# Softplus operations of the first group given a priority 250 instructions ahead, in a fused attention and mixture-of-experts kernel

## The chip, the cores and the metric

The kernel runs on one core of a Trainium2 chip. The metric is the device time of one execution in microseconds, the median over several runs; lower is better.

## What is computed

The reference is a chain of three stages over 4608 tokens of width 512.

```python
# 1. attention, keys and values averaged over windows of 8 (72 of 576 stay)
scores = q @ mean8(k).T / 8;  attn = softmax(scores);  x = attn @ mean8(v)
# 2. a dense layer with softplus
h = x @ w_in                                    # 512 -> 2048
g = maximum(h, 0) + log1p(exp(-abs(h)))
x = g @ w_out                                   # 2048 -> 512
# 3. tokens with x @ w_skip > 0 go through one of 8 experts (argmax of x @ w_gate)
h = maximum(x @ w1[e], 0);  out = x + gate * (h @ w2[e])
```

## The kernel before

Stage 2 goes over nine groups of 512 tokens, and in each over 16 chunks of 128 hidden columns. For a chunk, `p1` (L707 to L726) multiplies the group's activations `xh`, `xl` with a slice of `w_in`: 12 matmuls (L715) into one of two PSUM buffers `h`. Operands are split in a high and a low float32 part, and three products are summed. Then come seven instructions, which this text calls the softplus: Abs, Exp and Ln on ScalarE (L718, L719, L720), a combination on VectorE that reads `h` a last time (L721), a copy to the high part `gh` on ScalarE (L723) and the low part `gl` on VectorE (L725). `p2` (L728 to L738) multiplies `gh`, `gl` with a slice of `w_out`: 12 matmuls into the four accumulators `y`. In program order `p2` of a chunk follows `p1` of the chunk two further on. The next `p1` but one can't begin before L721 has read its `h` buffer.

Beside this, while group g is in stage 2, a generator `unit` (L622 to L670) per head pair makes the attention output of group g+1; four head pairs fill the `xh`, `xl` that the next group's `p1` reads, head pair by head pair (`kk` in the loop). One unit goes: load the keys (`kv<-kT`, L624, on SP's queue), reduce them over windows (`kp`, L530), copy them into a block-diagonal tile (`kbd`, L537, L538), scores on TensorE (`s`, L635), maximum and subtraction (L644, L645), Exp on ScalarE (L542), sums and a division, a transposition on VectorE (L653), twelve small copies that finish the transposition (`et<-q`, L659, on SP's queue), the product with the values (`o`, L569), and the split into `xh` (L571, ScalarE) and `xl` (L572, VectorE). The values are loaded (`kv<-vT`, L532), reduced (`vr`, L553), transposed on TensorE (`pv`, L560) and copied (`vp`, L562). There is one buffer each for `kv`, `et`.

While the first group runs, the weights of stage 2 are also unpacked for the first time: loads of 1 MB (L506) and, for each, two unpacking passes on ScalarE (L469, L471), two joins on VectorE (L474, L476), a copy to the high part (L519) and a subtraction (L520). Later groups reuse the tiles.

The order on each engine is not the program's. A scheduler places each instruction by a priority (its place in the program) among those that its model of the machine holds ready at that time; the engines then run what they were given strictly in that order and wait with semaphores. `tc.high_priority(offset=n)` gives the instructions inside it a priority as if they stood n places earlier. Stage 3 is ordered by hand and comes after all groups.

Of the kernel before, what the change touches and what calls it, by code (L numbers as in the profile page):

```python
# [9 lines left out]
F32 = mybir.dt.float32  # L10
F32R = mybir.dt.float32r
# [3 lines left out]
AF = mybir.ActivationFunctionType  # L15
ALU = mybir.AluOpType
# [4 lines left out]
P = 128  # L21
# [5 lines left out]
G = 512  # L27
# [2 lines left out]
XW = 520  # L30
BIG = float(1 << 20)
LAG = 2


@with_exitstack
def tile_kernel(ctx, tc, qT, kT, vT, wbits, w9, w1, w2, out):
    nc = tc.nc
# [382 lines left out]
    with ExitStack() as ph:  # L420
# [3 lines left out]
        gp = ph.enter_context(tc.tile_pool(name="gp", bufs=3))  # L424
        ap = ph.enter_context(tc.tile_pool(name="ap", bufs=2))
# [37 lines left out]
        def load_weights():  # L463
# [15 lines left out]
            def half(c, j, first):  # L479
                wh, wl = (wt[c // 2][:, c % 2, i, j * 512:(j + 1) * 512] for i in range(2))  # L480
                if first:
                    raw = room("raw", 1024, True).bitcast(I32).rearrange("p (a b) -> p a b", b=2)
                else:
                    raw = scratch.tile([P, 512, 2], I32, tag="raw", name="raw")
                nc.sync.dma_start(out=raw.rearrange("p a b -> p (a b)"),
                                  in_=bits[c * P:(c + 1) * P, j * 1024:(j + 1) * 1024])
                lo, hi = raw[:, :, 0], raw[:, :, 1]
                unpack(lo, hi)
                yield
                join(lo, lo, hi)  # L490
                nc.scalar.activation(out=wh, in_=lo.bitcast(F32), func=AF.Copy)
                yield
                nc.vector.tensor_tensor(out=wl, in0=lo.bitcast(F32), in1=wh.bitcast(F32),
                                        op=ALU.subtract)
                yield
# [3 lines left out]
            for c in range(EARLY):  # L499
                for j in range(2 if c >= LAG else 1):  # L500
                    yield from half(c, j, True)
            for i in range(EARLY // 2, 8):
# [14 lines left out]
                for j in range(2):  # L517
# [3 lines left out]
                    yield  # L521
            for c in range(LAG):
                yield from half(c, 1, False)
# [183 lines left out]
        def p1(g, c):  # L707
            xh, xl = X[g]
            w = wt[c // 2][:, c % 2]
            h = ps_h.tile([P, G], F32, tag="h", name="h")  # L710
            n = 0
            for kk in range(4):
                wh, wl = w[:, 0, kk * P:(kk + 1) * P], w[:, 1, kk * P:(kk + 1) * P]
                for l, r in ((wh, xh), (wh, xl), (wl, xh)):
                    nc.tensor.matmul(h, lhsT=l, rhs=r[:, kk, :], start=n == 0, stop=n == 11)  # L715
                    n += 1
            a = ap.tile([P, G], F32, tag="a", name="a")
            nc.scalar.activation(out=a, in_=h, func=AF.Abs)  # L718
            nc.scalar.activation(out=a, in_=a, func=AF.Exp, scale=-1.0)  # L719
            nc.scalar.activation(out=a, in_=a, func=AF.Ln, bias=1.0)  # L720
            nc.vector.scalar_tensor_tensor(out=a, in0=h, scalar=0.0, in1=a, op0=ALU.max, op1=ALU.add)  # L721
            gh = gp.tile([P, G], F32R, tag="gh", name="gh")
            nc.scalar.activation(out=gh, in_=a, func=AF.Copy)  # L723
            gl = gp.tile([P, G], F32R, tag="gl", name="gl")
            nc.vector.tensor_tensor(out=gl, in0=a, in1=gh.bitcast(F32), op=ALU.subtract)  # L725
            return gh, gl  # L726

        def p2(g, c, gh, gl):  # L728
            if c == 0:
                yps[g] = [ps_y.tile([P, D], F32, tag=f"y{t}", name=f"y{t}") for t in range(T)]  # L730
            w = wt[(c + LAG) % 16 // 2][:, (c + LAG) % 2]
            wh, wl = w[:, 0, 512:], w[:, 1, 512:]
# [10 lines left out]
        def ready(c):  # L743
            if c < EARLY:
                return 3 * (2 * c - min(c, LAG)) + 3
            return 3 * (2 * EARLY - LAG) + 6 * ((c - EARLY) // 2) + 6

# [45 lines left out]
        for g in range(NG):  # L793
            if g + 1 < NG:
                feed.start(units_of(g + 1), 6)
            for c in range(16):
                late = c >= EARLY
                while loaded[0] < min(STEPS, ready(c)):
                    weights(1)
                pend.append((g, c, *p1(g, c)))  # L800
                weights(2 if late else 3)
                feed.tick()
                if len(pend) > 2:
                    item = pend.pop(0)
                    p2(*item)
                    if item[1] == 15:
                        ends.append(finish(item[0], yps[item[0]], lambda: ps_a, "pa"))
                if g == NG - 1:
                    last_group(c)
                weights(1 if late else 3)  # L810
                feed.tick()
                if loaded[0] == STEPS and "cm9" not in ws:
                    scratch_cm.__exit__(None, None, None)
                    ws["cm9"] = ctx.enter_context(tc.tile_pool(name="cm9", bufs=1, side="right"))
                    ws["junk"] = ws["cm9"].tile([P, D], BF16, name="junk")
                    fill = ws["cm9"].tile([P, NCOL], I32, tag="fill", name="fill")
                    nc.gpsimd.memset(fill, int(BIG))
                    nc.sync.dma_start(out=tab.rearrange("(p c) b -> p (c b)", p=P), in_=fill)
            assert loaded[0] == STEPS
            while g + 1 < NG and (feed.units or jobs or ends):  # L820
                feed.tick()
# [17 lines left out]
        g = NG - 1  # L839
# [126 lines left out]
def _layout(q, k, v, moe_w_in, moe_w_out, moe2_w_skip, moe2_w_gate, moe2_w1, moe2_w2):  # L966
# [7 lines left out]
    def words(a, b):  # L974
# [3 lines left out]
            a.reshape(a.shape[0] // P, P, n, P).transpose(2, 1, 0, 3).reshape(n, P, -1),  # L978
            np.roll(b.reshape(n, P, -1), LAG, axis=0)], axis=2)).view(np.int64).reshape(n * P, -1)

# [30 lines left out]
```

## Time and profile before

| what | us |
|---|---|
| median of 3 runs (1370.27 to 1371.11) | 1370.47 |
| the profiled execution | 1378.22 |
| its span, first to last instruction | 1376.5 |
| TensorE busy in the span | 1338.4 (97%) |
| VectorE, ScalarE, GpSimd busy | 847.6, 594.6, 309.6 |

TensorE is the bound. It is busy to 90% or more in all of the span's 40 slices but the first two and the last two, so time can be won or lost only where it waits. Of the 38.1 us that it is not busy, 10.7 lie before 20 us, 7.5 between 20 and 140 us, 2.2 between 800 and 1000 us and 17.2 after 1000 us; between 140 and 800 us it has none. The first group is in stage 2 from 35.6 to about 154 us.

### The profile page before, as it was taken

Reading aid. Unit: us, or ns where it says so; the run is one execution under the profiler, and the core shown is the slowest. Engines: PE = TensorE matmul, PEld = TensorE weight load, DVE = VectorE, ACT = ScalarE, POOL = GpSimd, SP = SyncE. Lnnn points to the kernel's source line nnn. Section 1 sums busy time; section 2 is a strip of 40 time slices with the busy share of each in tenths; the row PEclk is TensorE's granted clock in tenths of the full one; section 3 lists DMA queues with packets and bytes.
Section 4 is the critical chain, followed back from the end, with each engine's and each line's share of the span. In section 5 each row is a group of like instructions: output and inputs, shape, how many; then the busy total and the mean of one; then the engine's idle time right before and its main releaser. Section 6 shows DMA issues by size and latency. Waiting matters only on the chain. (4 is left out here: it accounts for less than half of the span.)

```text
span 1376.5 us, 21364 instructions
## 1 busy us (share of the span) xinstructions
PE 1338.4 (97%) x7030; PEld 1114.9 (81%) x7030; DVE 847.6 (62%) x1951; ACT 594.6 (43%) x1076; POOL 309.6 (22%) x374
## 2 busy tenths in 40 slices
PE   6899999999999999999999999999999999999986
PEld 5667877777878778788778778888989898889886
DVE  7997794783974974965956847545645332325254
ACT  6985544544545545455455445541111121114142
POOL 2000012111121121030030120343424243323233
PEclk9999999999999999999999999999999999999998
DMA  8633343241241340431421301513323122225272
GB/s 283 260 115 90 86 136 75 59 130 48 76 125 35 80 129 26 112 106 31 118 70 33 106 13 47 192 39 92 96 70 100 57 76 67 81 61 169 64 269 80
DMA packets 149599, 134.16 MB, mean 97 GB/s; under 512 B 100789, under 2 KB 116789, under 8 KB 146912
## 3 DMA queue, kind: packets, MB, share of 16 engines
q1 hardware_dynamic: 131744, 95.51, 24.0%
q0 software_dynamic: 17728, 37.13, 8.5%
q8 instruction: 59, 0.97, 0.3%
q14 instruction: 68, 0.56, 0.1%
HBM read 166.67 MB, written 29.67 MB: 143 GB/s over the span
## 5 line engine op out<-in xcount | busy, mean ns | idle before, releaser
L715 PE MATMUL h<-xh,wt 128*128 128x512 f32 x1152 | 381.9, 393 | 3.4 <-DVE a L721 3.1
L715 PEld LDWEIGHTS h<-xh,wt 128*128 128x128 f32 x1152 | 217.6, 189 | 51.2 <-DVE a L721 4.9
L894 PE MATMUL h<-xt,w1h 128*128 128x256 f32 x1280 | 229.1, 282 | 4.2 <-ACT w1h L404 1.7
L736 PE MATMUL y<-wt,gh 128*128 128x512 f32 x576 | 233.2, 405 | 0.0
L119 DVE CUSTOM_DVE_ANT_0 junk<-rows,w9b 128x512 bf16<-128x512 f32 x324 | 223.0, 688 | 8.3 <-ACT rows L113 3.2
L715 PE MATMUL h<-xl,wt 128*128 128x512 f32 x576 | 225.7, 392 | 0.0
L737 PE MATMUL y<-wt,gh 128*128 128x512 f32 x576 | 225.4, 391 | 0.0
L738 PE MATMUL y<-wt,gl 128*128 128x512 f32 x576 | 224.7, 390 | 0.0
L894 PEld LDWEIGHTS h<-xt,w1h 128*128 128x128 f32 x1280 | 197.7, 189 | 9.2 <-issue 4.8
L894 PE MATMUL h<-xt,w1l 128*128 128x256 f32 x640 | 180.4, 282 | 3.8 <-issue 2.4
L898 ACT ACTIVATE hs<-h 128x512 fp32r<-128x512 f32 x80 | 47.6, 598 | 307.5 <-PE h L894 170.1
L718 ACT ACTIVATE a<-h 128x512 f32<-128x512 f32 x144 | 85.9, 597 | 184.1 <-PE h L715 172.4
L721 DVE SCALAR_TENSOR_TENSOR a<-h,a 128x512 f32<-128x512 f32 x144 | 98.5, 684 | 101.0 <-ACT a L720 100.4
L723 ACT ACTIVATE gh<-a 128x512 fp32r<-128x512 f32 x144 | 90.8, 630 | 158.5 <-DVE a L721 152.9
L736 PEld LDWEIGHTS y<-wt,gh 128*128 128x128 f32 x576 | 108.1, 188 | 36.5 <-ACT a L718 8.3
L715 PEld LDWEIGHTS h<-xl,wt 128*128 128x128 f32 x576 | 109.0, 189 | 22.9 <-issue 0.7
L738 PEld LDWEIGHTS y<-wt,gl 128*128 128x128 f32 x576 | 108.1, 188 | 23.7 <-DVE gl L725 0.4
L725 DVE TENSOR_TENSOR gl<-a,gh 128x512 fp32r<-128x512 f32 x144 | 99.2, 689 | 42.0 <-ACT gh L723 39.4
L894 PEld LDWEIGHTS h<-xt,w1l 128*128 128x128 f32 x640 | 122.7, 192 | 2.8 <-issue 1.0
L737 PEld LDWEIGHTS y<-wt,gh 128*128 128x128 f32 x576 | 108.3, 188 | 20.1 <-issue 0.4
L920 PE MATMUL y<-w2h,hs 128*128 128x512 f32 x304 | 118.4, 390 | 0.3 <-issue 0.3
L919 PE MATMUL y<-w2l,hs 128*128 128x512 f32 x304 | 118.4, 389 | 0.2 <-issue 0.2
(197 smaller groups left out, 1728.0 us busy)
## 6 DMA issues: line engine op xcount, KB each, us to landing
w9b<-w SPq DMA_DIRECT2D x81, 256.0 KB
raw<-wbits SPq DMA_DIRECT2D x12, 1024.0 KB
x2d<-rows SPq DMA_DIRECT2D x36, 260.0 KB
et<-q SPq DMA_DIRECT2D x256, 32.0 KB
kv<-kT SPq DMA_DIRECT2D x28, 288.0 KB
kv<-vT SPq DMA_DIRECT2D x28, 288.0 KB
xm<-misc SPq DMA_DIRECT2D x160, 32.0 KB
misc<-misc SPq DMA_DIRECT2D x144, 32.0 KB
```

The lines of the kernel that those rows point to most:

```text
L119: nc.vector.tensor_tensor_reduce(out=ws["junk"], in0=rows[t][:, :D], in1=w9b[e], scale=1.0, scalar=0.0, op0=ALU.mult, op1=ALU.add, accum_o ...
L715: nc.tensor.matmul(h, lhsT=l, rhs=r[:, kk, :], start=n == 0, stop=n == 11)
L718: nc.scalar.activation(out=a, in_=h, func=AF.Abs)
L721: nc.vector.scalar_tensor_tensor(out=a, in0=h, scalar=0.0, in1=a, op0=ALU.max, op1=ALU.add)
L723: nc.scalar.activation(out=gh, in_=a, func=AF.Copy)
L725: nc.vector.tensor_tensor(out=gl, in0=a, in1=gh.bitcast(F32), op=ALU.subtract)
L736: nc.tensor.matmul(y, lhsT=th, rhs=wh, start=c == 0, stop=False)
L737: nc.tensor.matmul(y, lhsT=th, rhs=wl, start=False, stop=False)
L738: nc.tensor.matmul(y, lhsT=tl, rhs=wh, start=False, stop=c == 15)
L894: nc.tensor.matmul(h[:, f2, :], lhsT=l, rhs=r[:, kk, :], start=n == 0, stop=n == 11)
L919: nc.tensor.matmul(y, lhsT=hh[:, f, js], rhs=ws["w2l"][:, f, :], start=False, stop=False)
L920: nc.tensor.matmul(y, lhsT=hl[:, f, js], rhs=ws["w2h"][:, f, :], start=False, stop=f == 7)
```

## The change

A constant AHEAD = 250 is added, and in the first group alone (`g == 0`) the seven instructions of a chunk's softplus are given a priority 250 places ahead. Nothing that is computed changes. Lines after the constant move down by one, those from the softplus on by four (L718 is L722 after the change).

```diff
+AHEAD = 250
...
-            a = ap.tile([P, G], F32, tag="a", name="a")
-            nc.scalar.activation(out=a, in_=h, func=AF.Abs)
...
+            with ExitStack() as st:
+                if g == 0:
+                    st.enter_context(tc.high_priority(offset=AHEAD))
+                a = ap.tile([P, G], F32, tag="a", name="a")
+                nc.scalar.activation(out=a, in_=h, func=AF.Abs)
+                nc.scalar.activation(out=a, in_=a, func=AF.Exp, scale=-1.0)
+                nc.scalar.activation(out=a, in_=a, func=AF.Ln, bias=1.0)
+                nc.vector.scalar_tensor_tensor(out=a, in0=h, scalar=0.0, in1=a, op0=ALU.max, op1=ALU.add)
+                gh = gp.tile([P, G], F32R, tag="gh", name="gh")
+                nc.scalar.activation(out=gh, in_=a, func=AF.Copy)
+                gl = gp.tile([P, G], F32R, tag="gl", name="gl")
+                nc.vector.tensor_tensor(out=gl, in0=a, in1=gh.bitcast(F32), op=ALU.subtract)
```

The scheduler makes of it other orders in the first group and at the step to the second; from `p2` of the second group's third chunk on TensorE's order is the old one but for one place.

ScalarE, around the Exp of the second head pair's attention (L542), before:

```order
L469 ACTIVATE raw_768<-raw_768 128x1024
L471 ACTIVATE raw_768<-raw_768 128x1024
L542 ACTIVATE q<-q 128x8x72
L571 ACTIVATE xh<-o 128x512
L538 ACTIVATE kbd_165<-kp 64x72
L723 ACTIVATE gh<-a 128x512
L469 ACTIVATE raw_905<-raw_905 128x1024
```

and after the change (L543 is the Exp, L572 `xh`, L727 `gh`, L722 Abs):

```order
L472 ACTIVATE raw_768<-raw_768 128x1024
L538 ACTIVATE kbd_165<-kp 64x72
L727 ACTIVATE gh<-a 128x512
L572 ACTIVATE xh<-o 128x512
L539 ACTIVATE kbd_165<-kp 64x72
L470 ACTIVATE raw_905<-raw_905 128x1024
L722 ACTIVATE a<-h 128x512
L543 ACTIVATE q<-q 128x8x72
L723 ACTIVATE a<-a 128x512
```

The Exp now stands behind `gh`, `xh`, a `kbd` copy, an unpacking pass and an Abs that it stood ahead of.

SP's queue, at the load of the keys of the third head pair (L624), before:

```order
L506 DMA raw_905<-wbits 128x2048 x2
L624 DMA kv<-kT 128x576
L659 DMA et<-q 32x8x32 x2
L659 DMA et<-q 8x8x32
L659 DMA et<-q 32x8x32 x2
```

and after (L625 is the load of the keys):

```order
L660 DMA et<-q 8x8x32
L660 DMA et<-q 32x8x32 x2
L660 DMA et<-q 8x8x32
L625 DMA kv<-kT 128x576
L626 DMA q<-qT 128x64
L626 DMA q<-qT 128x448
```

The load went from ahead of the second head pair's twelve copies to behind them. The load of the keys of the first unit for the third group moved in the same way, from ahead of the fourth head pair's copies to behind them.

TensorE, from the last `p1` matmuls of the second chunk of group 1 to `p2` of the first group's last chunk, before:

```order
L715 MATMUL h<-xl,wt_181 128x512
L715 MATMUL h<-xh,wt_181 128x512
L635 MATMUL s<-kbd_165,q 128x144
L635 MATMUL s<-kbd_167,q 128x144 x3
L736 MATMUL y_551<-wt_181,gh 128x512
```

and after, from the end of that `p2` to the beginning of the third chunk's `p1` (L570 is `o`, L636 `s`, L716 `p1`, L561 `pv`):

```order
L570 MATMUL o<-et,vp 64x64 x2
L636 MATMUL s<-kbd_165,q 128x144
L570 MATMUL o<-et,vp 64x448 x2
L636 MATMUL s<-kbd_167,q 128x144
L716 MATMUL h<-xh,wt_181 128x512 x2
L716 MATMUL h<-xl,wt_181 128x512
L716 MATMUL h<-xh,wt_181 128x512
L716 MATMUL h<-xl,wt_181 128x512
L716 MATMUL h<-xh,wt_181 128x512
L636 MATMUL s<-kbd_167,q 128x144 x2
L561 MATMUL pv<-ident,vr 72x128
L636 MATMUL s<-kbd_165,q 128x144
```

Now all of the first group's `p2` stand ahead of the fourth head pair's `o`, and behind it, with scores of the next unit between, the six matmuls that need this head pair (three of each of group 1's first two chunks). Before, `o` stood 8 `p2` and 15 `p1` matmuls ahead of `p2` of the last chunk.

## Rows read from the trace of the kernel before

**Rows 1.** Windows of 20 us: busy time of each engine, granted TensorE clock, DMA share, GB/s

```profile
60.00:80.00 20.00, 16.57 (x69) 11.70 (x67) 17.26 (x21) 19.32 (x31) 0.26 (x1) 0.91 0.52 179
80.00:100.00 20.00, 19.28 (x77) 14.26 (x77) 19.15 (x27) 15.64 (x26) 1.41 (x2) 0.91 0.33 89
```

**Rows 2.** Timeline of PE: start, us, line, operation; in brackets idle time before and releaser

```profile
62.55 0.50 PE L715 MATMUL h<-xh,wt 128*128 128x512 f32 x1 [2.03 <-DVE a L721]
...
64.49 1.05 PE L715 MATMUL h<-xh,wt 128*128 128x512 f32 x2
...
78.25 1.31 PE L569 MATMUL o<-et,vp 72*64 72x64 f32 x8 [0.96 <-PE s L635]
80.30 0.80 PE L715 MATMUL h<-xh,wt 128*128 128x512 f32 x1 [0.74 <-DVE a L721]
...
109.30 0.27 PE L560 MATMUL pv<-ident,vr 128*72 128x128 f32 x1 [0.98 <-DVE vr L553]
...
131.72 0.27 PE L560 MATMUL pv<-ident,vr 128*72 128x128 f32 x1 [0.76 <-DVE vr L553]
```

**Rows 3.** Timelines of ACT and DVE ahead of the first of these waits

```profile
58.45 2.00 ACT L519 ACTIVATE wt<-v 128x1024 fp32r<-128x1024 f32 x2
...
60.35 0.62 ACT L720 ACTIVATE a<-a 128x512 f32<-128x512 f32 x1
...
61.81 0.68 DVE L721 SCALAR_TENSOR_TENSOR a<-h,a 128x512 f32<-128x512 f32 x1
```

**Rows 4.** Timeline of ACT behind the second head pair's Exp

```profile
79.60 0.60 ACT L571 ACTIVATE xh<-o 128x512 fp32r<-128x512 f32 x1 [0.32 <-PE o L569]
...
81.03 1.17 ACT L469 ACTIVATE raw<-raw 128x1024 f32<-128x1024 f32 x1
```

**Rows 5.** Timeline of SP's queue: loads of keys, and the first of each unit's twelve copies

```profile
84.07 0.33 SPq L624 DMA_DIRECT2D kv<-kT  x1
87.29 8.61 SPq L659 DMA_DIRECT2D et<-q  x12
...
107.46 8.92 SPq L659 DMA_DIRECT2D et<-q  x12
116.49 0.38 SPq L624 DMA_DIRECT2D kv<-kT  x1
...
132.53 2.69 SPq L659 DMA_DIRECT2D et<-q  x4
```

**Rows 6.** Timelines of DVE and PE: the fourth head pair's keys and scores

```profile
119.53 0.75 DVE L530 TENSOR_REDUCE kp<-kv 128x72 f32<-128x576 f32 x1 [2.04 <-DMA kv<-kT]
...
121.27 1.39 PE L635 MATMUL s<-kbd,q 128*64 128x144 f32 x8
```

**Rows 7.** Timelines of PE and ACT: who passes whom on ScalarE

```profile
84.41 0.39 PE L715 MATMUL h<-xh,wt 128*128 128x512 f32 x1
...
86.33 0.27 ACT L562 ACTIVATE vp<-pv 72x128 f32<-72x128 f32 x1 [2.23 <-PE pv L560]
86.50 0.58 ACT L718 ACTIVATE a<-h 128x512 f32<-128x512 f32 x1
```

**Rows 8.** Timelines of PE, ACT and DVE at the step from group 0 to group 1

```profile
144.91 0.97 PE L569 MATMUL o<-et,vp 72*64 72x448 f32 x4
...
145.93 0.60 ACT L571 ACTIVATE xh<-o 128x512 fp32r<-128x512 f32 x1 [4.21 <-PE o L569]
146.56 0.69 DVE L572 SCALAR_TENSOR_TENSOR xl<-o,xh 128x512 fp32r<-128x512 f32 x1 [1.79 <-ACT xh L571]
...
146.85 0.39 PE L715 MATMUL h<-xh,wt 128*128 128x512 f32 x1
...
150.72 1.14 PE L635 MATMUL s<-kbd,q 128*128 128x144 f32 x8
...
156.92 0.39 PE L715 MATMUL h<-xh,wt 128*128 128x512 f32 x1
157.15 0.39 PE L736 MATMUL y<-wt,gh 128*128 128x512 f32 x1
```

More of the change, by code (lines that the diff above doesn't have):

```diff
@@ L716, in p1 @@
                     n += 1
-            a = ap.tile([P, G], F32, tag="a", name="a")
-            nc.scalar.activation(out=a, in_=h, func=AF.Abs)
[L719 to L725, printed above, removed]
+            with ExitStack() as st:
[10 more added lines that the diff above has]
+                nc.vector.tensor_tensor(out=gl, in0=a, in1=gh.bitcast(F32), op=ALU.subtract)
             return gh, gl
```

## The prediction, made before the changed kernel ran

> **What bounds the kernel now.** I looked first at the windows, for the stretches in which TensorE waits, then at its timeline there, then at the engines and the queue that release it. From 140 to 800 us TensorE has no idle time, so what the change does in the first group reaches the end as a plain shift, and the sum is the shift of one point on TensorE behind the change.
>
> In the first group there are two kinds of loss [rows 1, 2]. TensorE waits: 2.03 us for L721 to free an `h` buffer, 0.74 for the same, 0.96 around an `o`, 0.98 and 0.76 for `pv`; 5.5 us together. [...] (1 - 0.91) x 20 us is 1.8 us of full clock lost in each window, 3.6 at most. [...] The first wait shows why softplus is late: Ln at 60.35 stands behind two copies of new weights that take 2.00 us from 58.45 on, and L721 follows at 61.81 [rows 3].
>
> **What the change wins.** Softplus goes ahead of the unpacking, so the two waits for L721 and, I take it, both stretches of low clock go: TensorE would end group 0's work up to 5.5 + 3.6 = 9.1 us earlier, at least 2.8 + 1.8 (the waits for L721 and one stretch). No instruction is added or removed, on any engine or queue.
>
> **What it costs.** What softplus passes is also the attention for group 1, and this is a chain with little slack: `o` of the fourth head pair is at 144.91, `xl` at 146.56, and the first `p1` matmul that needs it starts at 146.85 between `p2` matmuls that still cover it [rows 8]. After the change all of group 0's `p2` stand ahead of this `o`, so nothing covers it. I follow the chain.
>
> - The second head pair's Exp stands behind four more operations and an Abs. From 79.60 to 82.20 the four take 2.6 us, the Abs 0.58 [rows 4, 7]: 3.2 us. Its twelve copies, at 87.29 before, would come at 90.5; less some 0.4 for TensorE being early, 90.1.
> - The keys of the third head pair were loaded at 84.07, ahead of these copies; now the load stands behind them on SP's queue. How such a period runs is in the rows of the next head pair, where the load stood behind the copies already: copies and load from 107.46 to 116.49, 9.0 us; `kp` 3.0 us later; `s` 1.7 us after that; first copy 11.3 us after that, at 132.53 [rows 5, 6]: 25.1 us. With the load ahead it was 107.46 - 87.29 = 20.2. The other row of twelve copies has 8.6 us for 8.9 [rows 5], so I take 24.9. Third head pair 115.0, fourth 139.9, against 132.53.
> - The keys of the next unit (for group 2) now stand behind the fourth head pair's copies too: loaded at 139.9 + 8.9 = 148.8, `kp` at 151.8, its `kbd` copies some 1.1 later, 152.9. ScalarE has `xh` of the fourth head pair behind them, though `o` could be done by 139.9 + 8.9 + 1 = 149.8 or little later. TensorE has a score of that unit ahead of the six `p1` matmuls too. They start at R = 153.4.
> - Before, `p2` of group 1 starts at 157.15 [rows 8]. From R to there the changed order still has 6 + 12 `p1` matmuls at 0.23 (4.1 us), three scores at 1.14 / 4 and a `pv` of 0.2 (1.05, of which 0.5 came later before), and a wait for `pv` and the score; nearest are 0.98 and 0.76 before each `pv` of rows 2, and I take 2.1 for both (bounds 0 and 3). So the shift is R + 4.1 + 1.05 + 2.1 - 0.5 - 157.15 = R - 150.4, or +3.0.
> - Before, `p2` of group 0's last chunk ends at 154.4 (157.15 less 12 matmuls at 0.23), with six `p1` matmuls, an `o` and four scores done that now come later (1.4 + 1.0 + 1.1). So TensorE runs out of work at 154.4 - 3.5 - 9.1 = 141.8 and, but for that `o` and two scores, waits to R. Such a wait is longer than all of rows 2, and I expect a stretch of low clock behind it as behind the first: up to 1.8 us, and a little on `o` and the scores in it. I take +2.0, bounds 0 and 5.
>
> The sum is +5.0. In the profiled execution that is 1378.2 + 5.0 = 1383.2; this execution lies 7.8 over the median, and I carry the shift over: 1370.5 + 5.0 = **1375.5 us**. R's bounds are 146.9 (both loads cost nothing, rows 8 as before) and 155 (25.1 twice, and no gain at the second head pair), so the shift is -3.5 to +4.6 before the clock.
>
> **A rule weighed.** ScalarE doesn't pass an operation that waits: a chunk's last matmul ended at 84.8, yet its Abs began at 86.50, behind a `vp` that stood 2.23 us for its `pv` [rows 7]. That is why I let `xh` wait for the `kbd` copies. If it could pass, R would be near 151.5 and the shift 1.9 less, +3.1. [...]
>
> **Rivals.**
> 1. *Attention keeps pace.* The loads of keys cost nothing where they stand, because the chain has another limit; R is 146.9 and the clock stays up: -3.5, 1367.0. For it speaks that from 87.29 to 107.46 a period was 20.2 us [rows 5]; against it, that this was the one period with the load ahead. It takes a fourth `o` at 145 or earlier. 8%.
> 2. *Gain and wait cancel.* The periods are 23 to 24 us, as SP's queue and VectorE are less crowded with softplus out of the way; R is 150 to 151.5 and the low clock costs 1: shift +0.6 to +2.1, about 1372. 20%.
> 3. *The clock stays low for the whole wait and well behind it.* Then `o` (0.97) and four scores (1.14) take twice as long ahead of R, and the 18 matmuls and the next ones lose 0.2 each: 2.1 + 3.6 in place of 2.0, shift +8.7, 1379. Rows 1 and 2 show low stretches that end soon after work goes on, against it; the wait is five times longer, for it. [...] 12%.
> 4. That the change does nothing is excluded: the orders differ on all engines.
>
> **How the numbers follow.** My forecast (+2.8 to +7) has 60%, with rivals 8, 20 and 12%. A measurement of this kernel can tell 0.2%, 2.7 us, from no change. So faster 8%, same 20%, slower 72%. The range goes from 1369.5, within rival 2's lower part and some of rival 1, to 1379.0, which holds most of rival 3.
>
> **What would show it.** In the changed kernel's trace no wait for L721 between 55 and 100 us and clock 1.00 there; the load of the third head pair's keys behind the copies, near 99 us; the fourth head pair's copies near 140; TensorE idle for some 9 us between 141 and 153, released by `o`'s copies, `kbd` and `xl`; clock under 1 in that window; from 175 us on the old pace, shifted by 3 to 7 us. I am wrong if the fourth head pair's copies begin before 136, or if TensorE's idle time between 140 and 160 us is under 7 us.

## The result and the profile after

| | before | after |
|---|---|---|
| median, us | 1370.37 (4 runs, 1369.67 to 1371.11) | 1378.4 (4 runs, 1378.13 to 1379.2) |
| ratio, 95% interval | | 1.0059 (1.0042 to 1.0077) |
| profiled execution, its span | 1378.22, 1376.5 | 1379.2, 1377.5 |

The change costs 8.0 us. Slower was forecast, by 5.0; 1378.4 lies in the range of 1369.5 to 1379.0, near the upper end, at the size of the third rival (1379).

The windows of the changed kernel, in 20 us as in [rows 1], and then in 5 us around the step from group 0 to group 1 (columns: window, busy time and instructions of PE, PEld, DVE, ACT, POOL, granted clock, DMA share, GB/s):

```profile
60.00:80.00 20.00, 19.46 (x88) 15.40 (x88) 17.27 (x21) 19.93 (x32) 0.26 (x1) 1.00 0.59 190
80.00:100.00 20.00, 19.32 (x89) 14.65 (x88) 18.74 (x24) 17.66 (x29) 1.97 (x1) 1.00 0.13 35
140.00:160.00 20.00, 10.72 (x34) 6.06 (x33) 9.66 (x25) 7.68 (x16) 0.26 (x1) 0.63 0.52 143
...
145.00:150.00 5.00, 1.56 (x8) 1.15 (x10) 0.62 (x2) 0.52 (x2) 0.00 (x0) 0.52 0.32 56
...
165.00:170.00 5.00, 5.00 (x22) 4.13 (x21) 3.18 (x8) 2.91 (x6) 0.53 (x1) 0.93 0.30 75
```

From 60 to 100 us the clock is now 1.00 where it was 0.91 twice, and of 60 to 80 us TensorE is busy 19.46 where it was 16.57. Then comes a hole that before did not have: of 140 to 160 us TensorE works 10.72, and the clock is 0.50 from about 145.2 to 165.7 us.

SP's queue in the changed kernel, loads of keys and the twelve copies, against [rows 5]:

```profile
91.92 8.59 SPq L660 DMA_DIRECT2D et<-q  x12
100.62 0.44 SPq L625 DMA_DIRECT2D kv<-kT  x1
...
116.19 8.21 SPq L660 DMA_DIRECT2D et<-q  x12
...
139.96 8.19 SPq L660 DMA_DIRECT2D et<-q  x12
148.25 0.38 SPq L625 DMA_DIRECT2D kv<-kT  x1
```

Every load of keys stands behind the copies of the unit ahead, and the fourth head pair's copies begin at 139.96 instead of 132.53. TensorE's timeline across the hole (start, us, line, operation; in brackets idle time before and its releaser), against [rows 8]:

```profile
145.34 0.48 PE L570 MATMUL o<-et,vp 72*64 72x64 f32 x4 [2.56 <-DMA et<-q]
...
149.70 1.76 PE L570 MATMUL o<-et,vp 72*64 72x448 f32 x4 [3.10 <-DMA et<-q]
152.59 0.85 PE L636 MATMUL s<-kbd,q 128*128 128x144 f32 x2 [1.13 <-ACT kbd L539]
153.21 1.22 PE L716 MATMUL h<-xh,wt 128*128 128x512 f32 x2
155.01 0.80 PE L716 MATMUL h<-xl,wt 128*128 128x512 f32 x1 [0.58 <-DVE xl L573]
...
159.71 0.40 PE L561 MATMUL pv<-ident,vr 128*72 128x128 f32 x1 [1.67 <-DVE vr L554]
...
160.58 0.80 PE L716 MATMUL h<-xh,wt 128*128 128x512 f32 x1
161.18 0.63 PE L716 MATMUL h<-xl,wt 128*128 128x512 f32 x1
...
165.80 0.40 PE L740 MATMUL y<-wt,gh 128*128 128x512 f32 x1
```

Five waits make 9.04 us. What stands between them is slow too: the last four matmuls of `o` take 1.76 us where they took 0.97, and `h` matmuls stand 0.43 us apart until 165.7, then 0.23. VectorE and ScalarE show the end of the chain:

```profile
151.14 0.75 DVE L531 TENSOR_REDUCE kp<-kv 128x72 f32<-128x576 f32 x1 [5.53 <-DMA kv<-kT]
...
151.99 0.26 ACT L538 ACTIVATE kbd<-kp 64x72 f32<-64x72 f32 x1 [4.82 <-DVE kp L531]
...
152.56 0.60 ACT L572 ACTIVATE xh<-o 128x512 fp32r<-128x512 f32 x1
...
152.91 0.69 DVE L120 CUSTOM_DVE_ANT_0 junk<-rows,w9b 128x512 bf16<-128x512 f32 x1 [1.02 <-DMA w9b<-w]
...
154.27 0.69 DVE L573 SCALAR_TENSOR_TENSOR xl<-o,xh 128x512 fp32r<-128x512 f32 x1
```

The last `o` of the hole ended at 151.46, yet `xh` began at 152.56, behind the `kbd` copies that waited for the next unit's keys. Then `xl` began only at 154.27, behind two reductions for the gates of stage 3 (L120) on VectorE, the first of which had waited for its weights until 152.91.

**A measure without the end of the program.** The n-th matmul of one trace is set beside the n-th of the profiled execution before; the difference of their starts is the shift. For the changed kernel it is -8.0 us at the 600th (147.1 us before), +5.8 at the 640th, and +8.33 from the 1400th (316 us) to the 4100th (900 us). So some 8 us were won in group 0, and 16.3 lost in the hole: 9.04 are the waits, and the other 7.3 the same work at a slower pace. In those TensorE counts as busy (5.00 us of 160 to 165, at a clock of 0.50), so time is lost not only where it waits. This says where the time lies, not what each part would give back: work done faster would in part only have waited longer for its inputs. At the end of this pair of executions only +1.1 us is left, while the medians differ by 8.0: the third stage differs between executions, and the first experiment is about that.

### The profile page after: what moved, and what is told of

Its sections match the earlier page's. It is cut to its first block, busy times and chain, and to the rows that moved or that the text cites. A ratio compares the mean times of both kernels' runs of the same rounds, so it can differ in the third digit from the quotient of the medians.

```text
span 1377.5 us, 21360 instructions
## 1 busy us (share of the span) xinstructions
PE 1339.0 (97%) x7030; PEld 1115.8 (81%) x7030; DVE 848.8 (62%) x1951; ACT 594.5 (43%) x1076; POOL 310.1 (23%) x374
## 5 line engine op out<-in xcount | busy, mean ns | idle before, releaser
L716 PE MATMUL h<-xh,wt 128*128 128x512 f32 x1152 | 382.2, 393 | 0.3 <-DVE xl L573 0.3
L716 PEld LDWEIGHTS h<-xh,wt 128*128 128x128 f32 x1152 | 217.7, 189 | 47.1 <-DVE xl L573 1.2
L120 DVE CUSTOM_DVE_ANT_0 junk<-rows,w9b 128x512 bf16<-128x512 f32 x324 | 222.3, 686 | 11.4 <-ACT rows L114 3.2
L716 PE MATMUL h<-xl,wt 128*128 128x512 f32 x576 | 226.1, 393 | 0.6 <-DVE xl L573 0.6
L722 ACT ACTIVATE a<-h 128x512 f32<-128x512 f32 x144 | 85.7, 595 | 198.1 <-PE h L716 197.6
L727 ACT ACTIVATE gh<-a 128x512 fp32r<-128x512 f32 x144 | 90.8, 630 | 153.9 <-DVE a L725 153.8
L716 PEld LDWEIGHTS h<-xl,wt 128*128 128x128 f32 x576 | 108.9, 189 | 24.3 <-DVE xl L573 1.3
L926 DVE SCALAR_TENSOR_TENSOR ys<-y,xg 128x512 f32<-128x512 f32 x38 | 28.5, 751 | 147.3 <-PE y L924 147.3
```

The source lines that it names most:

```text
L120: nc.vector.tensor_tensor_reduce(out=ws["junk"], in0=rows[t][:, :D], in1=w9b[e], scale=1.0, scalar=0.0, op0=ALU.mult, op1=ALU.add, accum_o ...
```

## The experiments

Theory 1: the hole comes from the order on SP's queue, where the load of a head pair's keys stands behind the copies of the one ahead. Theory 2, its rival: the softplus operations themselves hold back the attention's operations on ScalarE and VectorE. Theory 3 is about the size: of the 8.3 us some 5 are the clock. All results, with the shift at the 600th and the 4100th matmul (matmuls that an experiment adds are left out of the count):

| kernel | 600th | 4100th | ratio to before (95%) |
|---|---|---|---|
| the change | -8.0 | +8.33 | 1.0059 (1.0042 to 1.0077) |
| the change again (e11) | -7.8 | +8.83 | 1.0065 (1.0052 to 1.0077) |
| before again (e1) | +0.5 | +0.48 | one run, no ratio |
| keys ahead (e2) | -8.3 | -7.97 | 0.9961 (0.9948 to 0.9973) |
| keys from GpSimd's queue (e3) | -8.2 | -7.77 | 0.9938 (0.9920 to 0.9956) |
| keys from ScalarE's queue (e7) | -8.4 | -8.37 | 0.9964 (0.9951 to 0.9977) |
| Exp given priority (e4) | -8.1 | +7.07 | 1.0060 (1.0040 to 1.0079) |
| one load ahead (e8) | -8.0 | +6.48 | one run, no ratio |
| 100 places (e6) | -9.2 | -4.82 | 0.9962 (0.9949 to 0.9976) |
| before, keys ahead (e10) | -0.8 | -0.78 | 0.9991 (0.9981 to 1.0001) |
| wait filled (e5) | -8.4 | +5.24 | 1.0041 (1.0028 to 1.0054) |
| both waits filled (e9) | -8.6 | +3.41 | 1.0052 (1.0035 to 1.0069) |
| both filled again (e12) | -7.3 | +4.82 | 1.0055 (1.0041 to 1.0069) |

### The kernel before once more

No edit.

> The kernel before, unchanged, for a second trace. From 180 to 908 us the matmuls of the changed kernel came 8.33 us later than those of the profiled execution before, but by the end of that execution only 1.1 us later, since its last stage had waits of TensorE (38.56 us of work in 920 to 960, 19.70 in 1300 to 1320). If those waits belong to that one execution, this one takes 1370 to 1371 us and its matmuls from 1000 us on lie about 7 us ahead of that one's at the end; if they belong to the kernel, this execution is again near 1378.

It took 1383.28 us. Neither expectation holds as put: the first 900 us are the same within 1 us, and the third stage is longer still, by 4.7 us from the 4100th matmul to the last. Over all traces here that stretch runs from 7.3 us shorter to 7.3 us longer than in the profiled execution before, whatever was edited. The medians of the kernel before in the five comparisons were 1370.37, 1382.04 (beside e1 to e4), 1378.5 (e5 to e8), 1381.96 (e9, e10) and 1379.44 (e11, e12). So a time is compared only with before's runs beside it, and the shift at the 4100th matmul is the sharper number.

### The keys' loads out of the copies' way

Three edits of the changed kernel; e2 is

```diff
-                    nc.sync.dma_start(out=k, in_=kT[u])
+                    with ExitStack() as st:
+                        if g <= 2:
+                            st.enter_context(tc.high_priority(offset=AHEAD))
+                        nc.sync.dma_start(out=k, in_=kT[u])
```

and in e3 and e7 the load keeps its priority, but another engine issues it:

```diff
-                    nc.sync.dma_start(out=k, in_=kT[u])
+                    (nc.gpsimd if g <= 2 else nc.sync).dma_start(out=k, in_=kT[u])
```

(`nc.scalar` in e7).

> The changed kernel, with the loads of the keys of the next two groups' units also 250 places ahead. Theory 1 (the keys' load waits behind the twelve copies on SP's queue, so the fourth head pair is late and TensorE runs dry): the loads stand ahead of the copies, the fourth head pair's copies begin near 130 us as before (132.53), TensorE doesn't stop between 141 and 153 and keeps the 8.0 us that it was ahead at 139 us: 1370.4 - 8 = 1362.4, between 1361 and 1365. Theory 2 (the softplus operations hold back the attention's own operations on ScalarE and VectorE): their order is the changed kernel's, so the copies still begin near 92, 116 and 140 us, and the time stays at 1377 to 1379.

> The changed kernel, with the same loads at their own places in the program, but issued from GpSimd's queue, where they don't stand behind the copies. Theory 1: as with the loads ahead, 1362 to 1366 (GpSimd's own work may delay a load by one of its operations, some 1 to 2 us). Theory 2: nothing changes on ScalarE and VectorE, 1377 to 1379.

> The changed kernel, with the keys' loads of the next two groups' units issued from ScalarE's queue. Theory 1: as with GpSimd's queue, where the matmuls after 180 us came 8.25 us earlier than in the kernel before and the ratio was 0.9938: 7 to 9 us earlier, 0.993 to 0.996. The issues cost ScalarE, which is busy 19.9 of the 20 us from 60 to 80, some tenths of a us each; if that tells, the matmuls come 1 to 2 us later than with GpSimd's queue. Theory 2: 1.005 to 1.007.

SP's queue with the keys ahead (e2):

```profile
86.49 0.33 SPq L628 DMA_DIRECT2D kv<-kT  x1
88.62 8.60 SPq L663 DMA_DIRECT2D et<-q  x12
...
110.18 2.07 SPq L663 DMA_DIRECT2D et<-q  x3
112.35 0.38 SPq L628 DMA_DIRECT2D kv<-kT  x1
...
126.07 1.27 SPq L663 DMA_DIRECT2D et<-q  x2
```

and its window where the hole was:

```profile
140.00:160.00 20.00, 20.00 (x93) 16.30 (x92) 17.28 (x40) 13.30 (x27) 1.84 (x2) 1.00 0.41 114
```

The hole is gone in all three, with softplus at the priority that the change gave it, and the 8 us of group 0 stay won: the shift is -7.8 to -8.4. Theory 1 holds. The scheduler plans with the earlier loads, so the orders on TensorE, ScalarE and VectorE are others too; that the delay comes through the queue is read from the releasers in the changed kernel, the copies `et<-q` and the load `kv<-kT`. The fourth head pair's copies begin at 126.07. The times fall by 0.36 to 0.62%, between medians by 5 to 8 us; e2's median of 1376.9 beside 1382.04 is 5.1, 3 less than its shift. Part of that is the third stage, which in e2's profiled execution took 1.9 us more than in e1's. Issuing from ScalarE costs nothing that shows (-8.37 beside -7.77 from GpSimd). These three are versions that beat both kernels.

### The attention's Exp ahead as well

```diff
-            shares(e[:, :, :SP], sm, rc)
+            with ExitStack() as st:
+                if g == 1:
+                    st.enter_context(tc.high_priority(offset=AHEAD))
+                shares(e[:, :, :SP], sm, rc)
```

> The changed kernel, with the attention's Exp, sums, reciprocal and product of the next group's units also 250 places ahead, so that they don't stand behind softplus operations. Theory 2: the fourth head pair's copies come nearer to 132 us, and the time falls by a good part of the 8 us that was lost, to 1364 to 1372. Theory 1: the operations run earlier only where the keys have arrived, the copies stay near 92, 116 and 140 us, and the time stays at 1377 to 1380.

The shift is +7.07, the ratio 1.0060 is that of the change, and the copies begin at 92.00, 116.03 and 139.80. But the edit did not move the Exp: from 55 to 150 us ScalarE's order is that of the changed kernel, and on VectorE two reciprocals (L546) moved up by one place each. So e4 is no test of theory 2. What the traces themselves say of it, for the third head pair's Exp (L543), first in the changed kernel and in the last line in e4:

```profile
107.73 0.81 DVE L646 TENSOR_TENSOR q<-s,st 128x288 f32<-128x288 f32 x2
...
108.91 0.63 ACT L723 ACTIVATE a<-a 128x512 f32<-128x512 f32 x1
109.45 0.67 ACT L543 ACTIVATE q<-q 128x576 f32<-128x576 f32 x1
...
109.54 0.67 ACT L543 ACTIVATE q<-q 128x576 f32<-128x576 f32 x1
```

Its last input, the subtraction L646, was done at 108.54, and the Exp began 0.9 us later, behind a softplus Abs and Exp. The fourth's began 0.6 us after its input, behind `xh`. So on ScalarE softplus holds back the Exp by less than 1 us, in periods of 24.3 and 23.8. Theory 2 falls as the whole cause by e2, e3 and e7, where softplus has the same priority and the hole is gone; how much it adds where the keys are late was not tested.

### One load ahead, and 100 places in place of 250

e8 has e2's edit for the third head pair alone (`if g == 1 and hp == 2`). e6 is one number:

```diff
-AHEAD = 250
+AHEAD = 100
```

> The changed kernel, with one load alone ahead, that of the third head pair's keys. Theory 1: the load comes before the second head pair's copies, so that the third's begin 2 to 3 us sooner than in the changed kernel (near 113 instead of 116), but the load of the fourth head pair's keys still stands behind the third's copies, so its own copies begin at 135 to 139, TensorE still runs dry near 142 with a wait of 8 us or more in all, and the matmuls after 180 us are 4 to 8 us late. If one load out of order were the whole cause, they would be about 8 us early, as with all loads ahead.

> The change with 100 places ahead instead of 250. In SP's order all twelve copies of the second head pair then still stand ahead of one load of keys, but the load for the unit after is ahead of the third head pair's copies. Theory 1: the fourth head pair's copies begin at 125 to 133 us, TensorE has no wait over 3 us between 140 and 155, the waits of the first group (5.5 us) are gone, and the matmuls after 180 us come 5 to 8 us earlier than in the kernel before: 0.994 to 0.997 of its time. Theory 2 (the softplus operations on ScalarE and VectorE take the attention's places): fewer of them are ahead, so it expects part of the loss, 1.002 to 1.005.

In e8 the load came 7.6 us sooner than in the change, and the copies after it only 0.9 sooner. Its queue, and VectorE and ScalarE between:

```profile
93.01 0.55 SPq L628 DMA_DIRECT2D kv<-kT  x1
...
115.31 8.21 SPq L663 DMA_DIRECT2D et<-q  x12
```

```profile
101.49 2.35 DVE L521 TENSOR_TENSOR wt<-v,wt 128x1024 fp32r<-128x1024 f32 x2
...
105.19 0.69 DVE L729 SCALAR_TENSOR_TENSOR a<-h,a 128x512 f32<-128x512 f32 x1 [0.98 <-ACT a L728]
105.80 0.45 DVE L649 TENSOR_TENSOR q<-s,st 128x288 f32<-128x288 f32 x1
...
106.45 0.67 ACT L543 ACTIVATE q<-q 128x576 f32<-128x576 f32 x1
```

The subtraction that the third head pair's Exp needs (L649) stands behind two subtractions of the unpacking (L521, 2.35 us) and a softplus combination that waited 0.98 us for its Ln. So theory 2's mechanism exists at that spot, and together with the unpacking it takes most of what an earlier load gives: the copies were expected near 113 and came at 115.31. The shift of +6.48 is in the range that theory 1 gave. In e6 the load for the fourth head pair, at 111.31, is ahead of the third's copies, though the load before it is not; the fourth's copies begin 13.8 us behind the third's:

```profile
111.31 0.33 SPq L625 DMA_DIRECT2D kv<-kT  x1
113.04 8.21 SPq L660 DMA_DIRECT2D et<-q  x12
...
126.79 8.87 SPq L660 DMA_DIRECT2D et<-q  x12
```

126.79 was in theory 1's range, and the shift of -4.82 just under its 5 to 8. So of the two loads it is the fourth head pair's that decides, as far as e6 can tell, in which the softplus operations stand less far ahead as well. Of its 9.2 us it lost a part between 140 and 160 us, where TensorE was busy 17.81 of 20 us and the clock was 0.91.

### The keys ahead without the change

e2's edit in the kernel before.

> The kernel before (softplus at its own place) with the keys' loads alone 250 places ahead. If the gain of the versions with keys ahead (8 us earlier after 180 us) is that of softplus ahead, and the keys only keep it, this one keeps the waits of 2.03 and some 1 us on a at L721 between 60 and 81 us and the low clock there, and its matmuls come 0 to 2 us earlier: ratio 0.998 to 1.000. If the keys' loads bring the gain themselves: 5 to 8 us earlier, 0.994 to 0.996.

Its timeline of TensorE keeps waits for `a`, and the clock is under 1.00 in two of its windows, 0.96 from 60 to 80 us and 0.87 in the next:

```profile
62.50 0.50 PE L719 MATMUL h<-xh,wt 128*128 128x512 f32 x1 [0.70 <-DVE a L725]
...
79.88 0.79 PE L719 MATMUL h<-xh,wt 128*128 128x512 f32 x1 [2.95 <-DVE a L725]
```

```profile
80.00:100.00 20.00, 20.00 (x81) 15.32 (x82) 17.77 (x23) 15.38 (x25) 1.41 (x2) 0.87 0.24 59
```

The shift is -0.8. So the 8 us belong to softplus ahead; the keys only keep them.

### The hole filled with matmuls

e5 puts matmuls that nothing reads in TensorE's two waits for `o`, so that it works through them:

```diff
+        if g == 0:
+            for _ in range(30):
+                nc.tensor.matmul(yps[3], lhsT=wt[0][:, 0, 0, 0:P], rhs=X[0][0][:, 0, :], start=True, stop=True)
         w9b = [w9load(e) for e in range(4)]
```

> The changed kernel with 30 more matmuls (of 128x512, their result is read by nothing) at the end of the first group, 16 ahead of the first part of the last head pair's outputs and 14 ahead of the second, in the two waits of 2.56 and 3.10 us of TensorE. At 0.227 us each they take 3.6 and 3.2 us, so TensorE has about 1 us more of work than the waits hold. The keys' loads and copies are the changed kernel's. [...]

TensorE (L117 are the added ones, L573 is `o`, L719 is `h`):

```profile
143.01 3.92 PE L117 MATMUL y<-xh,wt 128*128 128x512 f32 x16 [0.69 <-ACT rows L114]
...
150.80 0.97 PE L573 MATMUL o<-et,vp 72*64 72x448 f32 x4
...
157.64 0.50 PE L719 MATMUL h<-xh,wt 128*128 128x512 f32 x1 [2.67 <-DVE a L728]
...
158.73 0.63 PE L719 MATMUL h<-xl,wt 128*128 128x512 f32 x1
...
162.07 0.40 PE L743 MATMUL y<-wt,gh 128*128 128x512 f32 x1
```

and one of its windows:

```profile
160.00:165.00 5.00, 5.00 (x19) 4.05 (x18) 3.20 (x9) 1.91 (x4) 1.42 (x1) 0.80 0.39 120
```

With theory 3, in which some 5 of the 8.3 us come of TensorE at a clock of 0.50 from 145.2 to 165.7 us, the clock would stay at 1.00 from 140 to 180 us and the shift be +1 to +4; with its rival, in which those 5 us are further waits for the chain of the next group's units, the shift would be +8 to +9.5 whatever the clock. The result fell between the two, +5.24. The clock stayed up through the filled waits (1.00 from 140 to 155 us), and `o` took 0.97 again. But then the third chunk's `p1` waited 2.67 us for softplus (L728) to free its `h` buffer, since the two chunks before it had got their last six matmuls only at 152.5 us, and behind this wait the clock was low once more, from 158.6 to 162.0 us. I had not counted that wait. e9 fills it too, with 14 more matmuls that need the last `xl` and so can't start earlier; 13 of them stand in this wait:

```diff
         yield
+        if g == 0:
+            for _ in range(14):
+                nc.tensor.matmul(yps[3], lhsT=wt[0][:, 0, 0, 0:P], rhs=X[1][1][:, 3, :], start=True, stop=True)
```

> The kernel with 30 more matmuls and 14 further ones after the last head pair's outputs, 13 of them in the wait of 2.67 us that was left there at 155.0 us (13 x 0.227 = 3.0 us), none of whose results is read. With the first 30 alone the matmuls after 180 us were 5.24 us late, the clock was 1.00 up to that wait and low from 158.7 to 162.1 us, in which 11 matmuls took 0.43 us instead of 0.227 (2.2 us). Theory 3 (the clock is the rest): no stretch under 1.00 from 140 to 180 us, and the matmuls after 180 us 5.24 - 2.2 + 0.5 = 3.5 us late, 2.5 to 4. Rival (the delay is the chain of softplus after the wait, whatever the clock): 5 to 6 us late.

```profile
152.24 0.73 PE L722 MATMUL h<-xh,wt 128*128 128x512 f32 x2 [0.70 <-ACT xh L578]
...
153.07 0.48 PE L722 MATMUL h<-xl,wt 128*128 128x512 f32 x1
...
154.48 3.25 PE L122 MATMUL y<-xl,wt 128*128 128x512 f32 x13
157.57 0.40 PE L722 MATMUL h<-xh,wt 128*128 128x512 f32 x1
...
160.53 0.39 PE L746 MATMUL y<-wt,gh 128*128 128x512 f32 x1
```

```profile
140.00:160.00 20.00, 18.62 (x85) 13.85 (x86) 10.96 (x27) 8.79 (x19) 0.26 (x1) 1.00 0.42 124
```

The shift of +3.41 is the one expected by theory 3 (3.5). Up to 163 us e5 and e9 have the same order on every engine but for the added matmuls, so the pair shows what the low clock costs. The third chunk's twelve `p1` matmuls take 4.43 us in e5 (157.64 to 162.07) and 2.73 in e9 (157.57 to 160.53, less one added matmul of 0.23): 1.7 us. In the changed kernel the same twelve, which wait for nothing between them, take 5.22 (160.58 to 165.80): 2.5 us of its 8.3 are the clock.

More is not shown. From the 600th to the 4100th matmul the changed kernel loses 16.3 us (16.6 in e11) and e9 12.05 (12.08 in e12), but those 4.2 us are not the clock's alone. With the added matmuls the scheduler made another order at the step: `xh` stands ahead of the `kbd` copies on ScalarE, `xl` ahead of the two reductions on VectorE, and the next `pv` behind `p2` of group 1's first chunk on TensorE:

```profile
151.59 0.60 ACT L578 ACTIVATE xh<-o 128x512 fp32r<-128x512 f32 x1 [3.61 <-PE o L576]
...
152.22 0.69 DVE L579 SCALAR_TENSOR_TENSOR xl<-o,xh 128x512 fp32r<-128x512 f32 x1 [1.02 <-ACT xh L578]
```

From the first `xh` matmul to `p2` it is 12.59 us in the changed kernel (153.21 to 165.80) and 8.06 in e9 (152.24 to 160.53, less the added 0.23). Of the 4.5 between them 2.5 are the twelve matmuls; 1.0 is the order, since the first `xl` matmul comes 1.80 us behind the first `xh` matmul there and 0.83 here; the 1.1 that is left holds matmuls at the slower pace (0.43 us apart from 155.60 to 156.46 in the changed kernel) and changes of order that no run separates. So the clock costs 2.5 to 3.6 us, and theory 3's 5 is too much.

The time, however, was 1.0052 of before's, not the 1.0025 that 3.4 us would make. It and the changed kernel were run once more, side by side:

> The changed kernel once more, on the same chip as the next one, since the third stage (from 908 us) takes up to 15 us more in some executions than in others: 1.0059 of the time before, as first measured (1.004 to 1.008), with matmuls after 180 us 8 us late.

> The kernel with both waits filled once more, whose matmuls after 180 us were 3.4 us late, but whose time was 1.0052 of before's. If the third stage has nothing to do with what comes before it, its time lies about 4.9 us (8.3 - 3.4) under that of the changed kernel on the same chip, near 1.0025 (1.001 to 1.004); if the third stage gives back what is gained earlier, as the first measurement would have it, the two are equal to 2 us, near 1.005 to 1.006.

The medians are 1388.76 and 1386.26 beside 1379.44: 2.5 us apart, with intervals that overlap; the spans of the two profiled executions are 3.7 us apart (1387.6 and 1383.9), their shifts 4.0. The profiled pair passes the gain on to the end. That the medians pass on only 2.5 us is not settled; neither expectation is met by them. It touches the third stage, not the hole.

## Why the prediction was right, and where it was off

- *What the change wins.* Bounds 4.6 and 9.1 us; measured 8.0. The waits for L721 [rows 2] are gone, the clock is 1.00, and e10 shows that this is softplus ahead.
- *The chain.* The second head pair's copies were put at 90.1 and came at 91.92; the third's at 115.0 and 116.19, the fourth's at 139.9 and 139.96; `kp` at 151.8 and 151.14, the `kbd` copies were to be done by 152.9 and were by 152.54, R was put at 153.4 and measured 153.21. That `xh` waits behind the `kbd` copies is as weighed [rows 7]: 152.56. That the loads' place on SP's queue carries this chain is confirmed by e2, e3 and e7, which change it and with it lose the hole. That the fourth's copies came within 0.1 us of the forecast is in part luck: the second's began 1.8 us later than put, and the two periods, 24.3 and 23.8, were 0.6 and 1.1 shorter than 24.9. One reading was too simple: I charged both periods with the load's place, 24.9 for 20.2. With the loads ahead they were 21.6 and 15.9 (e2): the third's stays nearly as long, with VectorE busy 18.87 us of 80 to 100 in e2, and the load's place tells in the fourth's.
- *From R to group 1's `p2`.* 6.75 us by the terms put there, which include 2.1 of waits; TensorE's two waits there were 0.58 and 1.67. Measured 12.59 (153.21 to 165.80). In e9, at the full clock and with `xl` sooner, it is 8.06. So about 1.3 us are a wait for softplus to free an `h` buffer for the third chunk, which was not in the sum; 1.0 is `xl` behind the two reductions on VectorE, not in the sum either; and 2.5 to 3.6 are the clock.
- *The clock: the step that failed, a term too small.* "I expect a stretch of low clock behind it as behind the first: up to 1.8 us, and a little on `o` and the scores in it. I take +2.0, bounds 0 and 5." I took the length of the stretch from [rows 1], where the waits were under 2.1 us and the matmuls behind them ran on without another. In that trace the clock is 0.50 from 63.0 to 66.4 and from 80.1 to 83.5 us, 3.4 us each time, and 1.00 in the rest of 60 to 90 us; `h` matmuls start 0.43 us apart in the first stretch (64.06 and 64.49). Here the waits were 2.56, 3.10, 1.13, 0.58 and 1.67 us in a row; the clock stayed low to 165.7, 12.5 us after `p1` had resumed, and cost 2.5 to 3.6. It lay inside the bounds. With the 1.3 and 1.0 above, this covers the way from the forecast's +5.0 to the measured +8.3: the direction and the chain were right, the size was 3.3 us short.
- *Rival 3* had the long stretch at the low clock, with 18 matmuls that lose 0.2 us each; in the changed kernel they start 0.43 us apart (155.60 to 156.03), where it is 0.23 at a clock of 1.00 [rows 8]. That its +8.7 is near the measured +8.3 is in part luck. It charged 2.1 us for slow `o` and scores ahead of R, which cost nothing: `o` was done at 151.46, and `xh` stood behind the `kbd` copies until 152.56. And it had no term for softplus and `xl`. In the change the clock is 0.50 from 145.2, and the wait of 2.56 us ended at 145.34; in e5, after the wait of 2.67 us, matmuls ran on from 157.64 and the clock fell at 158.6. So the stretch began with the end of the wait in one and 1 us behind it in the other; why it begins or ends is not shown by any run.
- *Rivals 1 and 2* needed the fourth head pair's `o` at 145 or a period of 23 to 24 us with little loss; the last part of `o` was at 149.70 and the periods 24.3 and 23.8, but with a hole as forecast.
- *Signs.* No wait for softplus's `a` from 55 to 100 us, the load near 99 (100.62), copies near 140, TensorE idle for 9 us of 140 to 160, the clock under 1: as said. One failed, "from 175 us on the old pace, shifted by 3 to 7 us": it is 8.33.

## What to carry to other kernels

When operations are given priority in a static order, look at what they push behind something slow on every queue, the DMA issue queue first: here loads whose turn came some 8 us later, behind twelve copies that together take 8.2 to 8.6 us on that queue, turned 8 us of gain into 8 of loss, and issuing them elsewhere kept the gain. Moves whose gain is an engine's earliness only shift the point at which it needs its next input, so ask when that input comes before counting the gain. And price a new hole in TensorE's work at more than its waits: in this one 9.0 us of waits came with 7.3 us of work at a slower pace, and twelve matmuls behind the waits took 5.22 us instead of 2.73. Before an experiment is read as a test of one thing, compare the orders that the scheduler made of it: in e4 the operation did not move, and in e5 and e9 others moved too.

## What was not expected

- The clock stayed at 0.50 for 20.5 us, in 14 of which TensorE was at work, and for 6 us after the last wait, that before `pv` at 159.71. After the single wait of 2.67 us in e5 it was low from 158.6 to 162.0 us. After waits of 0.69 and 0.70 us in e9 it was 1.00 (140 to 180 us).
- Matmuls that compute nothing made the real ones earlier: 44 of them, 10 us of TensorE's time, took 4 to 5 us off the shift, 1.0 of it by the other order that came with them.
- The same kernel before had medians from 1370.4 to 1382.0 us in the five comparisons. Its two traces agree up to 900 us within 1 us; what differs in them is the third stage.
